# Tiles 4 to 15 of x arrive transposed and are normalized with broadcast mean and scale tiles (gated linear-attention block, one core)

## The chip, the core and the metric

The kernel runs on one core of a Trainium2 chip. Its engines are PE (TensorE, matmuls and transposes), DVE (VectorE), ACT (ScalarE), POOL (GpSimd) and SP (SyncE, which here issues DMAs). Each engine works through its own queue in order; they meet through semaphores. The metric is device time in microseconds (us) of one execution. A profile is one execution recorded by the hardware profiler; its clock starts at the span's start.

## The reference

Input x is 2048 rows of 576 features, float32. Cut to what matters:

```python
xn = (x - mean(x)) / sqrt(var(x) + 1e-5)          # per row
q, k, v = split(xn @ wqkv)                        # 32 heads of 18
pq, pk = phi(q), phi(k)                           # phi(t) = (t+1 if t > 0 else exp(t)) + 1e-6
kv, z = pk^T v, sum(pk)                           # per head, over all rows
s = ((pq @ kv) / (pq . z + 1e-6)) @ wo
g = silu((gelu(xn @ w_gate) * (xn @ w_up)) @ w_down)
out = x + s * g
```

## The kernel before

The 2048 rows are 16 tiles of 128 tokens, four to a block, four blocks (tb 0 to 3) in two halves s = 0 and 1. Matmuls contract over features, so the normalized x is needed with features on the partitions. The 576 features are two halves of 288, and a half is three groups of 128 columns: two whole ones, and one of 32 that the host repeats four times (`xe`). A float32 operand is kept as two float32r words, a high one (an ACT copy) and the rest (a DVE subtraction), in the tiles `xo`; the plain float32 values lie in `xf`, because sums of blocks are formed from them later.

The stages, in order of time: the tile loop over x (K and V by `x_mm` and `kv_tile`, tiles 0 to 7), the Q products of blocks 0 and 1 (`q_store`), tiles 8 to 15, Q of blocks 2 and 3 (`q_hold`), the attention output (`s_mm`), the gate and up matrices (a seven-product block scheme, `matrix`), and the down projection (`down_all`) with the gating of the output in its last passes. The order of every engine's queue is the order in which the program is written (`pin`).

What happens to tile n of x, by the names that the profile shows:

- `load_x` (L153) brings a pair of tiles from `xe`, tokens on partitions, 768 columns each, into slot b14 or b15. From tile 4 on it waits until the slot's last pair is read.
- `spread` (L162) takes mean and variance on DVE (`bn_stats`, `bn_aggr`), with Ln and Exp on ACT; `scales` (L177) refines the scale on DVE.
- `center` (L192) subtracts and scales the tile in place, one DVE instruction over 128x768.
- `turn` (L198) makes six PE transposes of 128x128 into two PSUM banks, `xt`.
- `place` (L207) makes the operand's high words from the banks on ACT, and the rests on DVE.
- `save` (L224) copies the same banks to `xf` on ACT.

In `kv_tile(t)` (L433) the PE order is `x_mm(t, 0)`, `turn(t + 1)`, `x_mm(t, 1)`, `x_mm(t, 2)`, `kv_mm(t - 1)`; then comes `x_mm(t + 1, 0)`, the first to read the new operand. Each `x_mm` is 14 matmuls, 7 for each half of the features. Of the 7, the first four read the high words and the fifth and sixth the rests. On DVE the order is `k_post(t, 0)` (e_k and pk, 128x416), `place`'s subtractions, `k_post(t, 1)`, and then the mean, scale and centering of a later tile.

The passage from tile 7 to tile 8 I call the turnover. Eight `q_store` and one shorter one follow each other there, each with two ACT instructions and one DVE instruction (`phi`, written e_q and ph in the profile), and between them the list `behind` (L1347) puts the statistics of tiles 8 to 11, the preparation of tile 8, and `form` (L1344) of the block sums T1, T3 and T2. One `form` is a 128x1536 ACT copy, a DVE subtraction of 128x1024 and one of 32x512 (written xo_T), and a DMA of 1280 KB to DRAM (kept_T). All three use slot b12, so a `form` starts when the DMA of the one before has been read out. T1 to T4 replace the tiles of `xf` in place, and tile 8's new `xf` tiles take the slots of T1 and T3.

At the start 34 transposes of the identity (`idle`, L1230) run on PE while the first tile is loaded and normalized. At the end (`down_all`, L1197 to L1219) the last pass runs tile by tile (j = 0 to 3), and `close_last` (L1134) adds the PSUM bank to the accumulator (DVE), applies Silu (ACT), multiplies, adds x (DVE), and stores. For j = 3 it does all this in two halves of 144 columns.

Of the kernel before, what the change touches and what calls it, by code (L numbers as in the profile page):

```python
# [8 lines left out]
F32 = mybir.dt.float32  # L9
# [7 lines left out]
P = 128  # L17
# [70 lines left out]


@with_exitstack  # L90
def block_kernel(ctx, tc, x, xe, wq_d, wkv_d, wo, wgu_d, wd_d, out):
    nc = tc.nc
    sb = ctx.enter_context(tc.tile_pool(name="sb", bufs=1))

# [3 lines left out]
    def bank(name):  # L98
        return ps.tile([P, 512], F32, tag="one", bufs=6, name=name)
# [4 lines left out]
    def big(i, shape, dt, name):  # L104
        return sb.tile(shape, dt, tag=f"b{i}", bufs=1, name=name)
# [15 lines left out]
    def act(*args, **kw):  # L121
        pin(nc.scalar.activation(*args, **kw))  # L122

    def vec(op, *args, **kw):
        pin(getattr(nc.vector, op)(*args, **kw))  # L125
# [7 lines left out]
    def dma(out, in_, eng=None):  # L133
        tc.keep_in_program_order((eng or nc.sync).dma_start(out=out, in_=in_))
# [18 lines left out]
    def load_x(n, k):  # L153

        if n % 2 == 0:
            xstat[n // 2] = big(14 + n // 2 % 2, [P, 2, 2, 3 * P], F32, f"x_{n}")
        dma(
            out=xstat[n // 2][:, n % 2 : n % 2 + k],
            in_=xe[n * P : (n + k) * P].rearrange("(t p) j d -> p t j d", p=P),
        )  # L160

    def spread(n0, n):  # L162

        bn = sb.tile([P, TT, 12], F32, tag="bn", bufs=2, name=f"bn_{n0}")
        mv = sb.tile([P, 2 * TT, 2], F32, tag="mv", bufs=4, name=f"mv_{n0}")
        for t in range(n):
            xs = xstat[(n0 + t) // 2][:, (n0 + t) % 2]
            for j in range(2):
                vec("bn_stats", out=bn[:, t, 6 * j : 6 * j + 6], in_=xs[:, j, 0:HALF])
            vec("bn_aggr", out=mv[:, t, :], in_=bn[:, t, :])  # L170
        st = sb.tile([P, 6, TT], F32, tag="st", bufs=4, name=f"st_{n0}")
        act(st[:, 0, 0:n], mv[:, 0:n, 1], AF.Ln, bias=eps_t)
        act(st[:, 2, 0:n], st[:, 0, 0:n], AF.Exp, scale=-0.5)
        vec("tensor_scalar", st[:, 1, 0:n], mv[:, 0:n, 1], LN_EPS, None, op0=ALU.add)
        mom[n0] = n, mv, st

    def scales(n0):  # L177

        n, mv, st = mom.pop(n0)
        v, r, c = (st[:, i, 0:n] for i in range(1, 4))  # L180
        if n == 1:
            vec("tensor_scalar", c, r, r, -0.5, op0=ALU.mult, op1=ALU.mult)
            vec("tensor_scalar", c, c, v, 1.5, op0=ALU.mult, op1=ALU.add)
            vec("tensor_scalar", c, c, r, None, op0=ALU.mult)
        else:
            vec("scalar_tensor_tensor", c, r, -0.5, r, op0=ALU.mult, op1=ALU.mult)
            vec("tensor_mul", c, c, v)
            vec("scalar_tensor_tensor", c, c, 1.5, r, op0=ALU.add, op1=ALU.mult)
        for t in range(n):
            scale_of[n0 + t] = mv[:, t, 0:1], c[:, t : t + 1]  # L190

    def center(n):  # L192

        xs = xstat[n // 2][:, n % 2]
        m, r = scale_of.pop(n)
        vec("tensor_scalar", xs, xs, m, r, op0=ALU.subtract, op1=ALU.mult)

    def turn(n, new=bank):  # L198

        xs = xstat[n // 2][:, n % 2]  # L200
        tiles = [new(f"xt_{n}_{j}") for j in range(2)]
        xts[n] = [t[:, 0 : 3 * P].rearrange("p (k t) -> p k t", k=3) for t in tiles]
        for j in range(2):
            for k in range(3):
                pin(nc.tensor.transpose(xts[n][j][:, k, :], xs[:, j, k * P : (k + 1) * P], ident))  # L205

    def place(n, js=(0, 1), words=(0, 1)):  # L207

        tb, t = divmod(n, TT)
        s, b = divmod(tb, 2)  # L210
        c = slice(t * P, (t + 1) * P)
        for j in js:
            nm = BS[b][j]
            if nm not in xo[s]:
                xo[s][nm] = big(2 * b + j, [P, 5, TBN], F32R, f"xo_{s}_{nm}")
            o, v = xo[s][nm], xts[n][j]
            if 0 in words:
                act(o[:, 0:3, c], v, AF.Copy)
            if 1 in words:
                vec("tensor_sub", o[:, 3:5, c], v[:, 0:2, :], o[:, 0:2, c].bitcast(F32))  # L220
                r = slice(KR, 2 * KR)
                vec("tensor_sub", o[r, 2, c], v[r, 2, :], o[r, 2, c].bitcast(F32))

    def save(n, js=(0, 1), last=True):  # L224

        tb, t = divmod(n, TT)
        s, b = divmod(tb, 2)
        for j in js:
            nm = BS[b][j]
            if t == 0:  # L230
                at_ = XM[s][nm]
                xf[s][nm] = (mid if at_ < 3 else big)(at_, [P, 3, TBN], F32, f"xf_{s}_{nm}")
            act(xf[s][nm][:, :, t * P : (t + 1) * P], xts[n][j], AF.Copy)
        if last:
            xts.pop(n)
# [841 lines left out]
    def acc_of(o):  # L1077
        i, j = ACCS[o]
        if i not in acc_t:
            acc_t[i] = big(i, [P, 2, TT, HALF], F32, f"acc_{i}")  # L1080
        return acc_t[i][:, j]
# [49 lines left out]
        vec("tensor_add", t[:, 0], t[:, 0], t[:, 1])  # L1131
        stores.append(lambda: dma(out=out[rows(j), cols], in_=t[:, 0]))

    def close_last(o, j, p, parts):  # L1134

        _, cols, rows = places(o)
        w = HALF // parts
        y, t, b = acc_of(o)[:, j], sxs[o][j], banks[p % 2][j]
        d = dict(PROD[p][3])[o]
        cs = [slice(i * w, (i + 1) * w) for i in range(parts)]  # L1140
        for c in cs:
            vec("tensor_add" if d > 0 else "tensor_sub", y[:, c], y[:, c], b[:, c])
            act(y[:, c], y[:, c], AF.Silu, scale=float(SIGN[o]))

        def rest():
            for c in cs:
                z = t[:, 0, c]
                vec("tensor_mul", z, y[:, c], z)
                vec("tensor_add", z, z, t[:, 1, c])
                dma(  # L1150
                    out=out[rows(j), cols.start + c.start : cols.start + c.stop], in_=z
                )

        return [rest]

# [17 lines left out]
    def down_all():  # L1173
        late = []
        last = NP - 1
        for u in range(NP * NU):
            p, k = divmod(u, NU)
            n = KT * p + 2 * k
            for at in sorted(events):
                if at <= H_END + n // 2:  # L1180
                    run_events(at)
            if p in LOADS and k < 3:
                load_reg(*LOADS[p], k)
            if k == 0:
                for o, e in ENDS.items():
                    if e == p:
                        load_sx(o)
            if k < 2:
                change(p + 1, k)
                if p in SHARED:  # L1190
                    make_words(p + 1, k)
            elif k < 4:
                make_words(p + 1, k - 2)
                if p + 1 in SHARED and p:
                    make_words(p + 2, k - 2)
            cut(u + 2)
            if p == last and k == 2:  # L1197
                break
            for kt in range(*UNITS[k]):
                down_mm(p, kt, range(TT))  # L1200
            load_unit(p + 1, k)
            run(stores)
            if k == 1 and p:
                read(p - 1)
                late += [
                    lambda o=o, j=j: close(o, j) for o, e in ENDS.items() if e == p - 1
                    for j in range(TT)
                ]
            else:
                run(late, 2)  # L1210
        run(late)
        run(stores)
        o = next(o for o, e in ENDS.items() if e == last)
        for j in range(TT):
            for kt in range(UNITS[2][0], KT):
                down_mm(last, kt, (j,))
            late += close_last(o, j, last, 2 if j == TT - 1 else 1)
            run(late, len(late) - 1)
        run(late)  # L1219

# [6 lines left out]
        ins=[], outs=[], act_func_set_id=LN_EXP,  # L1227
    )))
    first = [own_bank(f"idle_{i}") for i in range(2)]
    for i in range(34):  # L1230
        pin(nc.tensor.transpose(first[i % 2][:, 0:P], ident, ident))  # L1231
    load_x(0, 1)
    load_kv(0, 0)
# [110 lines left out]
    def form(nm):  # L1344
        keep(0, nm, build(0, nm, 12))

    behind = {  # L1347
        (0, 0): [lambda: kv_mm(N0 - 1), lambda: spread(N0, 2), lambda: difference(0, 3)],
        (0, 1): [lambda: scales(N0), lambda: center(N0), lambda: q_store(1, 4)],
        (0, 2): [lambda: form("T1")],  # L1350
        (0, 3): [lambda: turn(N0), lambda: place(N0)],
        (1, 0): [lambda: form("T3"), lambda: save(N0)],
        (1, 1): [lambda: center(N0 + 1), lambda: spread(N0 + 2, 2), lambda: scales(N0 + 2)],
        (1, 2): [lambda: form("T2")],
    }
    for tb in range(2):
# [140 lines left out]
```

## Time and profile before

| quantity | value |
|---|---|
| time, median of 3 runs | 1473.43 us (1472.06 to 1473.94) |
| time of the profiled execution | 1472.68 us |
| span of the profiled execution | 1470.9 us |
| PE busy | 1461.8 us |
| DVE busy | 1138.0 us |
| ACT busy | 572.0 us |
| POOL busy | 579.1 us |
| granted PE clock, share of full speed | 0.999 |

The execution's time is 1.8 us longer than its span, which runs from the first to the last recorded work. Busy times overlap, so they don't add up to the span. In a timeline row the first number is the start, the second how long the row lasted (several instructions of one kind are merged, with their count at the end, and may overlap), and the brackets tell the idle time before it and what ended it. In the chain of waits, each row is the work that the next row waited for.

### The profile page before, as it was taken

To read this page: it belongs to the slowest core of one execution; us is meant where nothing else is said; L and a number is where in the kernel's file an instruction comes from. 1 tells how busy PE (TensorE), PEld (TensorE's weight loads), DVE (VectorE), ACT (ScalarE), POOL (GpSimd) and SP (SyncE) were. 2 spreads that over 40 slices of the span, in tenths; PEclk is the share of its full clock that TensorE was granted. 3 is DMA by queue.
4 is the path that set the end of the run, shared out by engine and by line. 5 is a ranking of instruction groups with operands and counts; after the bars stand their busy time and mean duration, and the time that the engine had idled before them with its cause. 6 is when DMAs were issued, how large, how long until landed. Compare 5 with 4: busy or idle time off the path is not lost.

```text
span 1470.9 us, 21966 instructions
## 1 busy us (share of the span) xinstructions
PE 1461.8 (99%) x8184; PEld 1303.9 (89%) x8184; DVE 1138.0 (77%) x1581; ACT 572.0 (39%) x936; POOL 579.1 (39%) x513
## 2 busy tenths in 40 slices
PE   9999999999999999999999999999999999999998
PEld 8989989988888888888888888888889999999998
DVE  7566477466878788877778888778788978989888
ACT  5445355433222332223223223322335556455444
POOL 3332340125655667655674755757632000000000
PEclk9999999999999999999999999999999999999999
DMA  4435004442242323334153242423379888767886
GB/s 175 157 135 204 5 2 180 147 189 86 93 144 97 125 87 116 128 115 136 51 172 100 94 136 73 157 87 101 128 271 345 270 258 253 244 190 233 278 287 216
DMA packets 116148, 230.43 MB, mean 157 GB/s; under 512 B 10874, under 2 KB 44410, under 8 KB 113994
## 3 DMA queue, kind: packets, MB, share of 16 engines
q1 hardware_dynamic: 113386, 216.97, 44.0%
q0 software_dynamic: 2656, 12.06, 2.2%
q8 instruction: 65, 1.06, 0.3%
q14 instruction: 41, 0.34, 0.1%
HBM read 146.37 MB, written 82.58 MB: 156 GB/s over the span
## 4 chain that ended last, share of the span: by engine, by line
PE 96%; DVE 2%; issue 1%; DMA 0%; ACT 0%; POOL 0%; ACTq 0%; DVEq 0%; POOLq 0%
PE bd L128 23%; PE ga L769 16%; PE al L769 16%; PE de L769 16%; PE kv L128 8%; PE be L769 8%; PE s L128 4%; PE q L128 3%; PE kv_a L128 1%; PE xt L205 1%; DMA raw_h<-hs 0%; PE idle L1231 0%; PE d L128 0%; PE kw L128 0%; DVE acc L125 0%
## 5 line engine op out<-in xcount | busy, mean ns | idle before, releaser
L131 POOL TENSOR_TENSOR sm<-raw 128x384 f32<-128x384 f32 x72 | 75.2, 1044 | 152.0 <-DMA raw<-in_wgu_dram 107.4
L128 PE MATMUL kv<-wkv,xo_B 128*128 128x388 f32 (+2 forms) x658 | 127.9, 349 | 0.5 <-DVE xo_B L125 0.4
L128 PEld LDWEIGHTS kv<-wkv,xo_B 128*128 128x128 f32 x658 | 118.8, 188 | 2.4 <-DVE xo_B L125 0.7
L125 DVE TENSOR_TENSOR wa<-sm,wa 128x768 fp32r<-128x768 f32 x72 | 92.5, 1285 | 36.1 <-ACT wa L122 35.2
L128 PE MATMUL bd<-w_head,hi 128*128 128x288 f32 x516 | 118.0, 294 | 0.0
L125 DVE TENSOR_TENSOR wb<-raw,wb 128x256 fp32r<-128x256 f32 (+1 forms) x108 | 107.0, 991 | 7.3 <-ACT wb L122 5.8
L125 DVE TENSOR_TENSOR wa<-raw,wa 128x256 fp32r<-128x256 f32 x72 | 68.2, 947 | 50.7 <-ACT wa L122 49.6
L122 ACT ACTIVATE hi<-raw_h 128x1024 fp32r<-128x1024 f32 x59 | 62.4, 1059 | 90.0 <-PE bd L128 60.9
L128 PE MATMUL bd<-w_end,hi 128*128 128x288 f32 x448 | 89.8, 294 | 0.0
L122 ACT ACTIVATE spot_h<-spot_h 128x512 f32<-128x512 f32 x49 | 30.8, 633 | 151.4 <-DVE spot_h L125 151.4
L128 PEld LDWEIGHTS bd<-w_head,hi 128*128 128x128 f32 x516 | 87.0, 188 | 0.1
L125 DVE TENSOR_TENSOR raw_h<-raw_h,hi 128x1024 fp32r<-128x1024 f32 x59 | 71.9, 1223 | 16.7 <-ACT hi L122 16.7
L128 PE MATMUL bd<-w_end,raw_h 128*128 128x288 f32 x264 | 77.9, 295 | 0.0
L122 ACT ACTIVATE u<-al 128x512 f32<-128x512 f32 x72 | 41.0, 592 | 90.0 <-PE al L769 60.9
L122 ACT ACTIVATE wa<-sm 128x1152 fp32r<-128x1152 f32 x36 | 41.8, 1161 | 84.8 <-PE de L769 84.8
L128 PEld LDWEIGHTS bd<-w_end,hi 128*128 128x128 f32 x448 | 71.9, 188 | 0.0
L128 PE MATMUL bd<-beside,raw_h 128*128 128x288 f32 x240 | 70.9, 295 | 0.0
L131 POOL TENSOR_TENSOR spot_h<-spot_h,spot_h 128x512 f32<-128x512 f32 x45 | 62.3, 1390 | 2.9 <-DVE spot_h L125 2.4
L769 PE MATMUL ga<-xo_B,wb 128*128 128x512 f32 x252 | 63.0, 389 | 0.0
L769 PE MATMUL al<-xo_B,wa 128*128 128x512 f32 x252 | 63.0, 389 | 0.0
L769 PE MATMUL al<-xr_B,wb 128*128 128x512 f32 x252 | 63.0, 389 | 0.0
L769 PE MATMUL al<-xr_B,wa 128*128 128x512 f32 x252 | 63.0, 389 | 0.0
(261 smaller groups left out, 4066.5 us busy)
## 6 DMA issues: line engine op xcount, KB each, us to landing
raw_h<-hs SPq DMA_DIRECT2D x176, 256.0 KB
raw<-in_wgu_dram SPq DMA_DIRECT2D x36, 768.0 KB
hs<-spot_h SPq DMA_DIRECT2D x90, 256.0 KB
hs<-spot_g SPq DMA_DIRECT2D x80, 256.0 KB
b<-in_wd_dram SPq DMA_DIRECT2D x42, 432.0 KB
hs<-spot_m SPq DMA_DIRECT2D x38, 256.0 KB
raw_g<-hs SPq DMA_DIRECT2D x22, 256.0 KB
kept_T<-xo_T SPq DMA_DIRECT2D x4, 1280.0 KB
```

The costliest lines, as they stand in the source:

```text
L122: pin(nc.scalar.activation(*args, **kw))
L125: pin(getattr(nc.vector, op)(*args, **kw))
L128: pin(nc.tensor.matmul(*args, **kw))
L131: pin(getattr(nc.gpsimd, op)(*args, **kw))
L205: pin(nc.tensor.transpose(xts[n][j][:, k, :], xs[:, j, k * P : (k + 1) * P], ident))
L769: nc.tensor.matmul(o, w[0:rows, wi, :], xop[0:rows, xi, :], start=(start and n == 0), stop=(n == len(PASSES) - 1), skip_group_check=True,)
```

## The change

For tiles 4 to 15 the host passes a second copy of x, `xt`, in which each tile stands with features on the partitions. `load_x` now loads both forms, 576 columns of the plain rows (for the statistics) and 768 columns of `xt`, in two DMAs. `center`, `save` and the six transposes fall away for these tiles. `turn` transposes two columns instead, the mean and the scale of the tile's tokens, each broadcast to 128x128, so that one PSUM bank `ms` holds both with tokens along the free axis. `normalize` subtracts the mean tile in place (128x768), multiplies by the scale tile into `xf` (twice 128x384), and makes the words from `xf` (`to_operand`, two ACT copies and four DVE subtractions). Tiles 0 to 3 stay as they were.

In the turnover, `form("T1")` moves from behind `q_store(0, 2)` to behind `q_store(0, 1)`, ahead of the shorter `q_store(1, 4)`, and tile 8 is prepared behind `form("T3")` instead of ahead of `q_store(1, 0)`.

The identity transposes at the start become 28. For j = 3 of the last pass, the accumulator is added to the PSUM bank ahead of the remaining matmuls of the pass, which then accumulate on top of it. Silu reads the bank, and the rest is done in one piece of 288 columns.

```diff
     def load_x(n, k):
         if n % 2 == 0:
-            xstat[n // 2] = big(14 + n // 2 % 2, [P, 2, 2, 3 * P], F32, f"x_{n}")
-        dma(
-            out=xstat[n // 2][:, n % 2 : n % 2 + k],
-            in_=xe[n * P : (n + k) * P].rearrange("(t p) j d -> p t j d", p=P),
-        )
+            shape = [P, 2, 2, 3 * P] if n < TT else [P, 2, D + 6 * P]
+            xstat[n // 2] = big(14 + n // 2 % 2, shape, F32, f"x_{n}")
+        t = xstat[n // 2][:, n % 2 : n % 2 + k]
+        if n < TT:
+            dma(out=t, in_=xe[n * P : (n + k) * P].rearrange("(t p) j d -> p t j d", p=P))
+        else:
+            dma(out=t[:, :, 0:D], in_=x[n * P : (n + k) * P].rearrange("(t p) d -> p t d", p=P))
+            dma(out=t[:, :, D:], in_=xt[n : n + k].rearrange("t p m -> p t m"))
...
     def turn(n, new=bank):
         xs = xstat[n // 2][:, n % 2]
+        if n >= TT:
+            xts[n] = t = bank(f"ms_{n}")
+            for i, v in enumerate(scale_of.pop(n)):
+                pin(nc.tensor.transpose(
+                    t[:, i * P : (i + 1) * P], v.to_broadcast([P, P]), ident
+                ))
+            return
...
+    def normalize(n, s, b, c):
+        ms = xts.pop(n)
+        xs = xstat[n // 2][:, n % 2, D:].rearrange("p (k t) -> p k t", k=6)
+        m, r = (ms[:, None, i * P : (i + 1) * P] for i in range(2))
+        vec("tensor_sub", xs, xs, m.to_broadcast([P, 6, P]))
+        for j, nm in enumerate(BS[b]):
+            if nm not in xo[s]:
+                xo[s][nm] = big(2 * b + j, [P, 5, TBN], F32R, f"xo_{s}_{nm}")
+                new_plain(s, nm)
+            vec(
+                "tensor_mul", xf[s][nm][:, :, c], xs[:, 3 * j : 3 * j + 3],
+                r.to_broadcast([P, 3, P]),
+            )
+        for nm in BS[b]:
+            to_operand(xo[s][nm], xf[s][nm], c)
...
+    def add_in(o, j, p):
+        b = banks[p % 2][j][:, 0:HALF]
+        vec("tensor_add" if dict(PROD[p][3])[o] > 0 else "tensor_sub", b, b, acc_of(o)[:, j])
...
+        if added:
+            act(y, b, AF.Silu, scale=float(SIGN[o] * d))
+        else:
+            vec("tensor_add" if d > 0 else "tensor_sub", y, y, b)
+            act(y, y, AF.Silu, scale=float(SIGN[o]))
...
         o = next(o for o, e in ENDS.items() if e == last)
+        add_in(o, TT - 1, last)
         for j in range(TT):
             for kt in range(UNITS[2][0], KT):
                 down_mm(last, kt, (j,))
-            late += close_last(o, j, last, 2 if j == TT - 1 else 1)
+            late += close_last(o, j, last, j == TT - 1)
...
-    for i in range(34):
+    for i in range(28):
...
     behind = {
         (0, 0): [lambda: kv_mm(N0 - 1), lambda: spread(N0, 2), lambda: difference(0, 3)],
-        (0, 1): [lambda: scales(N0), lambda: center(N0), lambda: q_store(1, 4)],
-        (0, 2): [lambda: form("T1")],
-        (0, 3): [lambda: turn(N0), lambda: place(N0)],
-        (1, 0): [lambda: form("T3"), lambda: save(N0)],
-        (1, 1): [lambda: center(N0 + 1), lambda: spread(N0 + 2, 2), lambda: scales(N0 + 2)],
+        (0, 1): [
+            lambda: scales(N0), lambda: form("T1"), lambda: q_store(1, 4),
+        ],
+        (0, 3): [lambda: turn(N0)],
+        (1, 0): [lambda: form("T3"), lambda: place(N0)],
+        (1, 1): [lambda: spread(N0 + 2, 2), lambda: scales(N0 + 2)],
         (1, 2): [lambda: form("T2")],
     }
```

More of the change, by code (lines that the diff above doesn't have):

```diff
@@ L90, in block_kernel @@
 @with_exitstack
-def block_kernel(ctx, tc, x, xe, wq_d, wkv_d, wo, wgu_d, wd_d, out):
+def block_kernel(ctx, tc, x, xe, xt, wq_d, wkv_d, wo, wgu_d, wd_d, out):
     nc = tc.nc
@@ L168, in spread @@
             for j in range(2):
-                vec("bn_stats", out=bn[:, t, 6 * j : 6 * j + 6], in_=xs[:, j, 0:HALF])
+                src = xs[:, j, 0:HALF] if n0 < TT else xs[:, j * HALF : (j + 1) * HALF]
+                vec("bn_stats", out=bn[:, t, 6 * j : 6 * j + 6], in_=src)
             vec("bn_aggr", out=mv[:, t, :], in_=bn[:, t, :])
@@ L200, in turn @@
         xs = xstat[n // 2][:, n % 2]
+        if n >= TT:
+            xts[n] = t = bank(f"ms_{n}")
[3 more added lines that the diff above has]
+                ))
+            return
         tiles = [new(f"xt_{n}_{j}") for j in range(2)]
@@ L205, in turn, with new_plain @@
                 pin(nc.tensor.transpose(xts[n][j][:, k, :], xs[:, j, k * P : (k + 1) * P], ident))
+    def new_plain(s, nm):
+        at_ = XM[s][nm]
+        xf[s][nm] = (mid if at_ < 3 else big)(at_, [P, 3, TBN], F32, f"xf_{s}_{nm}")
+    def normalize(n, s, b, c):
[13 more added lines that the diff above has]
+            to_operand(xo[s][nm], xf[s][nm], c)
     def place(n, js=(0, 1), words=(0, 1)):
@@ L211, in place @@
         c = slice(t * P, (t + 1) * P)
+        if n >= TT:
+            normalize(n, s, b, c)
+            return
         for j in js:
@@ L227, in save @@
         s, b = divmod(tb, 2)
+        if n >= TT:
+            return
         for j in js:
@@ L230, in save @@
             if t == 0:
-                at_ = XM[s][nm]
-                xf[s][nm] = (mid if at_ < 3 else big)(at_, [P, 3, TBN], F32, f"xf_{s}_{nm}")
+                new_plain(s, nm)
             act(xf[s][nm][:, :, t * P : (t + 1) * P], xts[n][j], AF.Copy)
@@ L1132, in close, with close_last @@
         stores.append(lambda: dma(out=out[rows(j), cols], in_=t[:, 0]))
-    def close_last(o, j, p, parts):
+    def add_in(o, j, p):
+        b = banks[p % 2][j][:, 0:HALF]
+        vec("tensor_add" if dict(PROD[p][3])[o] > 0 else "tensor_sub", b, b, acc_of(o)[:, j])
+    def close_last(o, j, p, added):
         _, cols, rows = places(o)
-        w = HALF // parts
-        y, t, b = acc_of(o)[:, j], sxs[o][j], banks[p % 2][j]
+        y, t, b = acc_of(o)[:, j], sxs[o][j], banks[p % 2][j][:, 0:HALF]
         d = dict(PROD[p][3])[o]
[L1140 to L1143, printed above, removed]
-        def rest():
[L1146 to L1152, printed above, removed]
+        if added:
[3 more added lines that the diff above has]
+            act(y, y, AF.Silu, scale=float(SIGN[o]))
+        def rest():
+            z = t[:, 0]
+            vec("tensor_mul", z, y, z)
+            vec("tensor_add", z, z, t[:, 1])
+            dma(out=out[rows(j), cols], in_=z)
         return [rest]
@@ L1482 @@
     for name, a in (
-        ("x", xs), ("xe", xe), ("wq", wq), ("wkv", wkv), ("wo", A_wo), ("wgu", wgu), ("wd", wd)
+        ("x", xs), ("xe", xe[0 : 4 * P]), ("xt", xt), ("wq", wq), ("wkv", wkv), ("wo", A_wo), ("wgu", wgu), ("wd", wd)
     ):
```

1 line of the change is left out of this document (added).

## The prediction

> **What bounds the kernel now.** I read the page's busy times and its chain first, then PE's own waits, then the groups of instructions by shape, and last the timeline of the places that the change touches.
>
> ```profile
> span 1470.9 us, 21966 instructions
> ...
> PE 1461.8 (99%) x8184; PEld 1303.9 (89%) x8184; DVE 1138.0 (77%) x1581; ACT 572.0 (39%) x936; POOL 579.1 (39%) x513
> ...
> PE 96%; DVE 2%; issue 1%; DMA 0%; ACT 0%; POOL 0%; ACTq 0%; DVEq 0%; POOLq 0%
> ```
>
> PE is busy for 1461.8 of 1470.9 us, and 96% of the chain that ended last is PE. It is idle for 9.1 us: some 5.3 follow its last matmul (the tail's rows below), and of the rest these are the waits that bear on the change:
>
> ```profile
> PE idle L1231 <- POOL ident masks.py:199: 1.8, 1, 1.8
> ...
> PE kv L128 <- DVE xo_B L125: 0.4, 1, 0.4
> ...
> PE xt L205 <- DVE x L125: 0.2, 1, 0.2
> ```
>
> The first is the start, before the first instruction. So an instruction taken out of PE's queue shortens the program by its pace, as long as no other engine then comes too late. That is the question for each part.
>
> **Transposes.** Their group among PE's instructions by shape:
>
> ```profile
> L205 PE MATMUL xt<-ident,x 128*128 128x128 f32 x96 | 13.2, 274 | 0.8 <-issue 0.5 <-DVE x L125 0.2
> ```
>
> 96 transposes (16 tiles of six) keep PE busy for 13.2 us, 0.1375 us each at their pace; the 274 ns of one overlaps its neighbours. Twelve tiles lose four each: 48 x 0.1375 = **6.6 us**. The two that stay in a tile read a broadcast column, which no row shows. Bounds: no dearer, or paced by the 188 ns of the slowest common weight load:
>
> ```profile
> L128 PEld LDWEIGHTS kv<-wkv,xo_B 128*128 128x128 f32 x658 | 118.8, 188 | 2.4 <-DVE xo_B L125 0.7
> ```
>
> That would be 24 x 0.05 = 1.2 us dearer. I take 0, since their shape and type are those of the transposes.
>
> **DVE in an ordinary tile.** The group rows for the instruction that goes (the centering, L125's TENSOR_SCALAR on x) and for subtractions of two tensors:
>
> ```profile
> L125 DVE TENSOR_TENSOR xo_B<-xt,xo_B 128x256 fp32r<-128x256 f32 x32 | 13.5, 422 | 3.0 <-ACT xo_B L122 2.3
> ...
> L125 DVE TENSOR_TENSOR xf_B<-xf_B,xf_B 128x1536 f32<-128x1536 f32 x6 | 12.6, 2098 | 0.3
> L125 DVE TENSOR_SCALAR x<-x,mv,st 128x768 f32<-128x768 f32 x16 | 10.9, 680 | 0.6
> ```
> ```profile
> L125 DVE TENSOR_TENSOR raw_h<-raw_h,hi 128x1024 fp32r<-128x1024 f32 x59 | 71.9, 1223 | 16.7 <-ACT hi L122 16.7
> ```
>
> From 422 ns at 256 elements to 1223 at 1024 is 1.04 ns an element, so 128x768 comes to 0.96 us and 128x384 to 0.56. In a tile DVE gains 0.96 + 2 x 0.56 = 2.08 us and loses the 0.68 of the centering; ACT loses the two copies of `save`. Whether PE then waits, the rows of tile 4 show: its turn, the end of `k_post` ahead of it on DVE, and the first matmuls that read it.
>
> ```profile
> 42.75 0.82 PE L205 MATMUL xt<-ident,x 128*128 128x128 f32 x6
> ```
> ```profile
> 43.46 0.58 DVE L125 TENSOR_SCALAR pk<-kv 128x416 f32<-128x416 f32 x1
> ```
> ```profile
> 49.49 2.88 PE L128 MATMUL kv<-wkv,xo_B 128*128 128x416 f32 x14
> ```
>
> DVE is free at 44.04. The subtraction lasts to 45.0, the first multiplication to 45.6, its ACT copy (0.49, as 128x384 takes in the turnover's rows) to 46.1. The first matmul would start at 49.49 - 0.55 (four transposes fewer) = 48.94. So 2.8 us of other matmuls cover the new work and I cost it at nothing; each microsecond beyond that cover would cost 11, once for every tile but 8.
>
> The Trainium skill (VectorE: DVE Perf Modes, section Why PSUM operands drop a tier) says that an operand in PSUM holds a float32 instruction at one element a cycle. That speaks against this change, for the centering it removes does 768 elements in 0.68 us, less than the 0.96 interpolated. At the centering's pace a multiplication would cost some 0.42 instead of 0.56, the chain of the turnover below would be about 1.0 us shorter, and the sum better by as much. By the rule, the rows of two tensors are the ones to go by, and the sum stays as it is.
>
> **Loads.** A pair now moves 576 KB more and takes one more SP issue. In the late tiles SP waits in `load_x` for DVE's multiplications instead of the transposes, some 3 us longer; queued behind it are stores of ph and kept_T, which nobody reads soon. For tiles 12 and 13, the issue and the first reader:
>
> ```profile
> 124.79 0.86 SPq L134 DMA_DIRECT2D x<-in_xe_dram  x1
> ```
> ```profile
> 140.38 0.82 DVE L125 BATCH_NORM_STATS2 bn<-x 128x6 f32<-128x288 f32 x2
> ```
>
> 15.6 us lie between: no cost. Were they used up, tile 12 would be late by the excess.
>
> **The turnover.** Here other work already ends last. The chain of waits before:
>
> ```profile
> 118.18 2.61 PE kv L128 x14
> ...
> 121.52 0.68 DVE xo_T L125
> ...
> 122.23 0.69 DVE ph L125
> 122.93 0.50 DVE e_k L125
> 123.42 0.50 DVE pk L125
> ```
>
> It leaves PE for DVE: T2's subtraction, ph, `k_post`, and then tile 9's words. That is PE's 0.4 + 0.2 = 0.6 us of waiting in the second fence. What holds T2 back stands further up, in ACT's queue, DVE's, and SP's:
>
> ```profile
> 95.32 0.64 ACT L122 ACTIVATE e_q<-e_q 128x512 f32<-128x512 f32 x1
> ...
> 106.10 0.63 ACT L122 ACTIVATE e_q<-e_q 128x512 f32<-128x512 f32 x1
> 109.30 1.49 ACT L122 ACTIVATE xo_T<-xf_B 128x1536 fp32r<-128x1536 f32 x1 [2.57 <-DMA kept_T<-xo_T]
> ...
> 112.84 0.49 ACT L122 ACTIVATE xf_B<-xt 128x384 f32<-128x384 f32 x1 [1.68 <-DVE xo_T L125]
> ```
> ```profile
> 110.82 1.92 DVE L125 TENSOR_TENSOR xo_T<-xf_B,xo_T 128x1024 fp32r<-128x1024 f32 x2 [4.03 <-ACT xo_T L122]
> ...
> 115.17 0.81 DVE L125 BATCH_NORM_STATS2 bn<-x 128x6 f32<-128x288 f32 x2
> ...
> 117.19 0.17 DVE L125 TENSOR_SCALAR st<-mv 128x2 f32<-128x2 f32 x1
> ```
> ```profile
> 103.41 0.32 SPq L134 DMA_DIRECT2D kept_T<-xo_T  x1
> ```
>
> T3's copy at 109.30 had waited 2.57 us for T1's DMA, issued at 103.41: a trip of 5.9. In the changed kernel T1 starts behind the e_q that ends at 95.96: copy 1.49, DVE 1.92 and a bit, issue near 99.6, read out by 105.5. So the trip no longer holds T3; ACT's queue does, until e_q of `q_store(1, 0)` ends at 106.73 - 0.55 (tile 8's shorter turn) = 106.2. T3 comes 3.1 us earlier. But tile 8's normalization now stands behind it, in front of everything else. In before's clock: T3's copy to 107.7, DVE to 109.6; subtraction and two multiplications to 111.6; the second ACT copy 0.49 and its words 0.75 (two of the four subtractions) to 112.9; ph 0.69 to 113.6; statistics of tiles 10 and 11, 2.02 (from 115.17 to 117.19), to 115.6; then on ACT the Ln and Exp 0.5, two e_q of 0.6, T2's copy 1.49, to 118.8; DVE 1.92 to 120.7; ph to 121.4; `k_post` 1.0 to 122.4; tile 9's subtraction and multiplication 1.52 to 123.9; ACT 0.49 to **124.4**. PE without waits: tile 9's first matmul stood at 118.18 + 2.61 + 2.61 x 388/412 (the last product's narrower columns) = 123.2; two shorter turns make it **122.1**. PE waits 2.3 us where it waited 0.6: a loss of **1.7 us**. From tile 10 on the ordinary cover holds again. Bounds: no wait at all (0.6 better than before), or a wait of 3.6 (3.0 worse than before), with DVE's pieces slowed as the 128x1536 rows are, 2.10 on average against 1.75 in the one below:
>
> ```profile
> 93.75 1.75 DVE L125 TENSOR_TENSOR xf_B<-xf_B,xf_B 128x1536 f32<-128x1536 f32 x1
> ```
>
> **Start.** The last idle transposes, then DVE's rows: the centering of tile 0, tile 1's weights and words; then PE ahead of tile 2's turn.
>
> ```profile
> 7.23 0.82 PE L1231 MATMUL idle<-ident 128*128 128x128 f32 x6
> ```
> ```profile
> 6.41 0.68 DVE L125 TENSOR_SCALAR x<-x,mv,st 128x768 f32<-128x768 f32 x1
> ...
> 11.18 1.61 DVE L125 TENSOR_TENSOR wkv<-rw,wkv 128x832 fp32r<-128x832 f32 x2
> ...
> 13.46 1.51 DVE L125 TENSOR_TENSOR xo_B<-xt,xo_B 128x256 fp32r<-128x256 f32 x4 [0.67 <-ACT xo_B L122]
> ```
> ```profile
> 25.68 0.54 issue
> ```
>
> The last six idle transposes take 0.82 us and tile 0 is ready at 7.09, before 7.23, so its turn comes 0.82 earlier. At 25.68 PE waits for tile 2, at the end of a nearly full DVE queue. That queue moves as far as tile 1's words do, and they can't start before DVE is free at 12.79, 0.67 before 13.46. I take **0.65**; bounds 0 and 0.82.
>
> **Tail.** DVE's adds, and PE's first matmul for j = 3:
>
> ```profile
> 1462.29 0.81 DVE L125 TENSOR_TENSOR acc<-acc,bd 128x288 f32<-128x288 f32 x2
> ...
> 1465.60 0.52 DVE L125 TENSOR_TENSOR acc<-acc,bd 128x144 f32<-128x144 f32 x2 [0.17 <-PE bd L128]
> ...
> 1467.80 0.31 DVE L125 TENSOR_TENSOR sx<-sx 128x144 f32<-128x144 f32 x1
> ```
> ```profile
> 1463.42 0.29 PE L128 MATMUL bd<-beside,hi 128*128 128x288 f32 x1
> ```
>
> DVE is nearly full from 1462.3 on and ends at 1468.1; the last store ends the span. The early add goes ahead of j = 0's, from 1462.3 to 1462.7, and delays the adds behind it by 0.4. PE reaches j = 3 at 1463.42, so 0.7 us cover it; without them PE would wait for it. Out go the two late adds (0.52), their wait (0.17), and, with one piece for two, some 0.3. Net **0.6**; bounds 0 (the last store is larger) and 0.9.
>
> **The sum.** 6.6 + 0.65 + 0.6 - 1.7 = 6.15 us. The profiled execution's own time is 1472.68, the span and 1.8 around it, so 1466.5. It lies 0.75 below the median of the runs, 1473.43; the forecast for a median is **1467.3**.
>
> **Rivals.**
> - *The turnover is cured.* T3's 3.1 us suffice and PE doesn't wait: 1467.3 - 2.3 = 1465.0. For it: the wait that held T3 goes. Against: what is put behind T3 is all in DVE's one queue.
> - *The turnover is worse and the transposes dearer*, both upper bounds: 1467.3 + 1.3 + 1.2 = 1469.8. For it: T1's trip has only 0.7 us of reserve, and POOL adds ph beside DVE there. Against: one of the two bounds has no row of its own.
> - *Every tile waits*, the slower side. If DVE took far longer over a broadcast PSUM operand, the first operand of each tile, priced at 1.52 us, would outlast its cover. That begins at 2.8 times my price; at 3.6 times the delay is 3.95, 1.15 over the cover, and costs 11 x 1.15 = 12.7: 1480.0. Against: no row of two tensors is that slow.
> - *The change doesn't do what it says*: PE's transposes hide a wait that comes to light when they go, and the time stays at 1473.4. Against: 0.6 us of waiting is all that PE shows at these tiles.
>
> **Chances.** The forecast 0.50, cured 0.20, worse 0.14, every tile waits 0.09, nothing gained 0.07. About 0.2% (2.9 us) is what a measurement can tell from no change. Faster takes in the first two and nearly all of the third, 0.80; same 0.11; slower 0.09. The range, 1464.5 to 1470.6, holds the first three cases with the bounds of their costs.
>
> **What would show it.** Right: PE's idle rows shorter by six, 24 transposes of ms at the pace of xt, a wait of 2 to 3 us on xo_B once near 122 and none at other tiles, DVE's last row ending some 0.6 sooner behind PE's last matmul. Wrong: waits on xo_B at many tiles, a wait on x's loads, or transposes of ms that are slower than those of xt.

## The result, and the profile after

| quantity | before | after |
|---|---|---|
| time, median of 13 runs each | 1472.30 us (1471.28 to 1473.94) | 1469.94 us (1467.89 to 1471.75) |
| ratio, 95% interval | | 0.998 (0.9972 to 0.9987) |
| profiled execution: time, span | 1472.68, 1470.9 us | 1467.89, 1466.2 us |
| PE busy, DVE busy in it | 1461.8, 1138.0 us | 1454.2, 1152.6 us |

The change makes the kernel faster by 2.4 us of the medians, 0.16%: the forecast direction, within the range, but 2.6 us above the forecast time and not beyond the 0.2% that was set as the bound for calling it faster. Of the rivals, the one nearest to it is the worse turnover with dearer transposes, 1469.8. The profiled execution gained twice as much, 4.8 us; it is one of the two fastest of the 13, and why that matters comes out below. Three lines of the page, in the form that was shown of before:

```profile
span 1466.2 us, 21844 instructions
...
PE 1454.2 (99%) x8130; PEld 1296.8 (88%) x8130; DVE 1152.6 (79%) x1602; ACT 561.1 (38%) x911; POOL 578.2 (39%) x513
...
PE 95%; DVE 3%; ACT 1%; issue 1%; POOL 0%; ACTq 0%; DVEq 0%; POOLq 0%
```

PE lost 7.6 us of busy time, the span only 4.7: PE's idle time rose from 9.1 to 12.0 us. Its waits (engine, tile and line, what released it; us in all, count, longest) say where:

```profile
PE kv L128 <- ACT xo_B L122: 2.6, 1, 2.6
...
PE xt L218 <- PE idle L1272: 0.8, 1, 0.8
```

One wait of 2.6 us stands at tile 9's first product, and no other tile waits for its operand. The second row is the start, where tile 0's turn now waits for the centering instead of standing in the queue.

**The transposes.** PE's instructions on the two broadcast columns, and DVE's of the normalization (each row: x count, busy us, mean ns, idle before):

```profile
L210 PE MATMUL ms<-ident,mv 128*128 128x128 f32 x12 | 3.3, 272 | 0.0
L210 PE MATMUL ms<-ident,st 128*128 128x128 f32 x12 | 3.3, 276 | 0.1
```
```profile
L125 DVE TENSOR_TENSOR xf_B<-x,ms 128x384 f32<-128x384 f32 x24 | 12.2, 550 | 0.4
L125 DVE TENSOR_TENSOR x<-x,ms 128x768 f32<-128x768 f32 x12 | 11.4, 951 | 0.3
```

A broadcast column costs what a plain transpose did (274 ns). The two DVE instructions were priced at 0.96 and 0.56 us and took 0.951 and 0.550. What a tile of x saves is best read in the chain of waits, where each row is the time that the work held the path. Before, then after, from one `turn` to the next:

```profile
42.91 0.66 PE xt L205 x6
43.57 5.10 PE kv L128 x28
48.67 0.88 PE kv_a L128 x8
...
52.37 0.66 PE xt L205 x6
```
```profile
42.11 0.22 PE ms L210 x2
42.33 5.11 PE kv L128 x28
47.44 0.88 PE kv_a L128 x8
...
51.13 0.22 PE ms L210 x2
```

The period falls from 9.46 to 9.02 us. All of it is in the transposes, 0.66 us for six and 0.22 for two, so 0.11 us each, and the matmuls between have the same times. Twelve tiles make 12 x 0.44 = 5.3 us.

**The turnover.** The rows of PE, ACT and DVE around tile 9's first product (in brackets the idle time before and what ended it):

```profile
122.47 2.90 PE L128 MATMUL kv<-wkv,xo_B 128*128 128x416 f32 x14 [2.63 <-ACT xo_B L122]
```
```profile
103.66 1.48 ACT L122 ACTIVATE xo_T<-xf_B 128x1536 fp32r<-128x1536 f32 x1
...
121.89 0.99 ACT L122 ACTIVATE xo_B<-xf_B 128x384 fp32r<-128x384 f32 x2 [4.13 <-DVE xf_B L125]
```
```profile
116.65 1.92 DVE L125 TENSOR_TENSOR xo_T<-xf_B,xo_T 128x1024 fp32r<-128x1024 f32 x2 [1.35 <-ACT xo_T L122]
118.60 0.69 DVE L125 TENSOR_SCALAR ph<-q 128x512 f32<-128x512 f32 x1
...
120.31 0.95 DVE L125 TENSOR_TENSOR x<-x,ms 128x768 f32<-128x768 f32 x1
121.30 1.02 DVE L125 TENSOR_TENSOR xf_B<-x,ms 128x384 f32<-128x384 f32 x2
```

The order is the one that was forecast: T2's subtraction, ph, `k_post`, tile 9's subtraction and multiplications, its copy, PE. T3's copy no longer waits for a DMA. By then this kernel is 2.5 us ahead of before's clock (the first e_q stands at 87.92 against 90.42), so T3 started at 106.16 on that clock, and 106.2 was forecast.

**The end and the middle.** PE's last matmul and DVE's last instruction:

```profile
1460.65 0.29 PE L128 MATMUL bd<-w_end,raw_g 128*128 128x288 f32 x1
```
```profile
1462.21 0.46 DVE L125 TENSOR_TENSOR sx<-sx 128x288 f32<-128x288 f32 x1
```

DVE ends 1.73 us behind PE's last matmul, 0.8 sooner than before (2.55), but the store that ends the span takes 3.5 us from there where the smaller one took 2.8. So the tail went from 5.34 to 5.26 us in this pair. The start of the down projection moved more than the end did, as the chain shows:

```profile
1092.62 138.23 PE bd L128 x1044
...
1230.87 6.83 DMA raw_h<-hs
```
```profile
1088.77 203.25 PE bd L128 x1535
```

At its start the kernel is 3.85 us ahead (1092.62 - 1088.77). Another 0.7 come up inside the down projection, 372.2 us against 372.9 to PE's last matmul, where before's chain left PE for a DMA at 1230.87 and after's runs on. The one edit in that stretch, the early add at its end, is not the cause: e3 and e8 below have the old end and take 372.2 too, while e4, the kernel before with another start, takes 372.9. In before and e4 PE waits there once for the words of raw_h, 0.2 us, and the weight loads wait 0.8 to 1.0 us for them; what makes them late was not tried. So of the profiled 4.8 us, about 4 belong to the edits: 0.77 at the start (the products behind tile 3's turn begin at 33.34 against 34.11), 5.3 from transposes, 2.0 lost to the wait (2.63 instead of 0.6), 0.1 at the tail: 4.2. The medians show 2.4. The question for the experiments was where the rest goes.

### The profile page after: what moved, and what is told of

Read it like the earlier page. It is cut to its first block, busy times and chain, and to the rows that moved or that the text cites. A ratio compares the mean times of both kernels' runs of the same rounds, so it can differ in the third digit from the quotient of the medians.

```text
span 1466.2 us, 21844 instructions
## 1 busy us (share of the span) xinstructions
PE 1454.2 (99%) x8130; PEld 1296.8 (88%) x8130; DVE 1152.6 (79%) x1602; ACT 561.1 (38%) x911; POOL 578.2 (39%) x513
## 4 chain that ended last, share of the span: by engine, by line
PE 95%; DVE 3%; ACT 1%; issue 1%; POOL 0%; ACTq 0%; DVEq 0%; POOLq 0%
PE bd L128 24%; PE al L807 16%; PE ga L807 16%; PE de L807 16%; PE be L807 8%; PE kv L128 7%; PE s L128 4%; PE q L128 3%; PE kv_a L128 1%; DVE sx L125 1%; PE d L128 0%; PE kw L128 0%; PE idle L1272 0%; PE b L128 0%; ACT xo_T L122 0%
## 5 line engine op out<-in xcount | busy, mean ns | idle before, releaser
L125 DVE TENSOR_TENSOR wb<-raw,wb 128x256 fp32r<-128x256 f32 (+1 forms) x108 | 101.0, 935 | 7.4 <-ACT wb L122 5.8
L807 PE MATMUL de<-xo_T,wa 128*128 128x512 f32 x252 | 63.0, 389 | 0.0
L807 PE MATMUL de<-xo_T,wb 128*128 128x512 f32 x252 | 63.0, 389 | 0.0
```

What stands on the lines that cost most here:

```text
L807: nc.tensor.matmul(o, w[0:rows, wi, :], xop[0:rows, xi, :], start=(start and n == 0), stop=(n == len(PASSES) - 1), skip_group_check=True,)
```

## The experiments

Each was timed beside runs of the kernel before on the same chip, whose medians in three batches were 1472.22, 1472.53 and 1472.70 us. The edits are made to the changed kernel unless said otherwise.

**e1: the turnover mended.** T2 is formed a tile later, behind tile 9's words, and T4 moves with it.

```diff
         (1, 1): [lambda: spread(N0 + 2, 2), lambda: scales(N0 + 2)],
-        (1, 2): [lambda: form("T2")],
     }
...
+        if n == N0:
+            ends.append(lambda: form("T2"))
-        if n == N0 + 1:
+        if n == N0 + 2:
             ends.append(lambda: form("T4"))
```

> The changed kernel with the forms of T2 and T4 one step later: T2 behind tile 8's products instead of ahead of the last q_store, T4 behind tile 10's instead of tile 9's, so that 3.4 us of ACT and DVE work no longer stand ahead of tile 9's words. Theory A (the wait of 2.63 us in the profile costs what it lasts and nothing else): the wait is gone, PE's row of it shows less than 0.5, and the median falls by 2 to 2.7 us below the changed kernel's 1469.9, to 1467.2 to 1467.9. Rival C (PE's wait also lets the granted clock fall in most executions, which the one profiled did not show): the median falls by 3.5 us or more, to 1466.4 or less, and the runs lie closer together. Rival D (the same work only makes a later tile wait): a wait on xo_B at tile 10 or 11 of 1 us or more, median within 1 us of 1469.9.

Measured: 1465.72 us (1465.05 to 1466.35), ratio 0.9955 (0.9943 to 0.9968). PE's waits:

```profile
PE xt L218 <- issue: 0.5, 1, 0.5
...
PE kv L128 <- ACT xo_B L122: 0.2, 1, 0.2
```

The wait shrank by 2.4 us, the median by 4.2. The wait seems to cost more than its own length. The two profiled executions, in which PE's granted clock is 1.00 in all tiles, lie 2.4 us apart (1465.52 against 1467.89), which is the wait and no more.

**e2: 34 idle transposes.** The start as it was before.

```diff
-    for i in range(28):
+    for i in range(34):
```

> The changed kernel with 34 identity transposes at the start as before, nothing else. Theory A (start worth what the profile shows, 0.77 us): the first matmul of the first tile comes 0.6 to 0.9 us later and the median is 0.5 to 1.0 us above the changed kernel's 1469.9. Rival B (with 28, PE is granted its full clock later in most executions, which costs more than the start gains): the median is 1 us or more below 1469.9.

Measured: 1471.04 us (1467.99 to 1471.78), ratio 0.9985 (0.9976 to 0.9994). That is 1.1 us above the changed kernel, within both kernels' spread, so it doesn't price the start. What the run showed lies elsewhere. Its 11 times fall into two groups, five from 1467.99 to 1468.72 us and six from 1471.04 to 1471.78. Its profile has the same wait as the changed kernel and another length of the product behind it:

```profile
123.34 4.25 PE L128 MATMUL kv<-wkv,xo_B 128*128 128x416 f32 x14 [2.62 <-ACT xo_B L122]
```

These 14 matmuls took 2.90 us above. PE by stretches of 2 us (window, length, PE busy and count, PE's granted clock, share and rate of the DMAs), here and then in the changed kernel:

```profile
120.00:122.00 2.00, 0.71 (x5) 1.00 0.97 410
122.00:124.00 2.00, 0.66 (x2) 0.72 0.90 366
124.00:126.00 2.00, 2.00 (x8) 0.50 0.74 169
126.00:128.00 2.00, 2.00 (x12) 0.93 1.04 397
```
```profile
120.00:122.00 2.00, 0.00 (x0) 1.00 0.98 410
122.00:124.00 2.00, 1.53 (x8) 1.00 0.85 240
124.00:126.00 2.00, 2.00 (x14) 1.00 0.87 220
```

While PE still waited, the granted clock began to fall, to 0.50 here; it stayed at 1.00 in the one profile of the changed kernel. PE's busy time times the share of the clock that was missing gives 0.66 x 0.28 + 2 x 0.50 + 2 x 0.07 = 1.3 us lost.

**e3: the old tail.** `close_last` and the last pass as before: no early add, j = 3 in two halves.

```diff
-        add_in(o, TT - 1, last)
...
-            late += close_last(o, j, last, j == TT - 1)
+            late += close_last(o, j, last, 2 if j == TT - 1 else 1)
```

> The changed kernel with the end as before: no early add into the bank, j = 3 closed in two halves. Theory A (the tail gained DVE time and gave it back in the larger last store, 5.26 us from PE's last matmul to the span's end against 5.34): median within 0.3 us of the changed kernel's 1469.9, span's end 5.2 to 5.5 us behind PE's last matmul. Rival (my forecast's 0.6 us for the tail): median 0.5 to 0.9 us above.

Measured: 1470.71 us (1468.56 to 1472.60), ratio 0.9989 (0.9980 to 0.9997). From PE's last matmul to the span's end there are 5.78 us against 5.26, more than was expected of a tail that gives its gain back. The median, 0.8 us higher, can't be put down to the tail alone, since most of these executions have a lower mean clock (0.997 or 0.998). In the profile, the fall of the clock began within the wait of 2.63 us and lasted longer than in e2:

```profile
120.00:122.00 2.00, 0.00 (x0) 0.96 0.98 410
122.00:124.00 2.00, 1.53 (x4) 0.50 0.75 235
124.00:126.00 2.00, 2.00 (x7) 0.50 0.93 258
126.00:128.00 2.00, 2.00 (x8) 0.50 0.97 389
128.00:130.00 2.00, 2.00 (x11) 0.83 0.05 18
```

By the same sum that is 3.1 us (the first row holds no matmul), more than the wait itself.

**e4: 28 idle transposes in the kernel before.** Its one edit is `range(34)` to `range(28)`.

> The kernel before with 28 identity transposes instead of 34, nothing else. Theory A: 0.6 to 0.9 us faster than before (median near 1471.6), with the transposes of tile 0 starting near 7.2 us. Rival B (clock granted later): no faster than before, or slower, with a pace of the first matmuls above that of before.

Measured: 1471.51 us (1470.72 to 1472.41), ratio 0.9995 (0.9986 to 1.0004): 0.7 us by the medians, and an interval that takes in no change.

**e5: the wait filled.** 22 idle transposes of the identity go between the two products, where PE waits. The wait for tile 9 itself is left as it is.

```diff
+    def fill():
+        t = bank("fill")
+        for i in range(22):
+            pin(nc.tensor.transpose(t[:, i % 2 * P : (i % 2 + 1) * P], ident, ident))
...
+        if n == N0:
+            ends.append(fill)
```

> The changed kernel, its turnover as it is, with 22 identity transposes put on PE where it waits for tile 9 (22 x 0.11 = 2.4 us of the 2.63), so that PE is idle for only some 0.2 us there while tile 9 comes no sooner. Theory C (the idle time lets the granted clock fall to half for 1 to 6 us in most executions): the clock stays at 1.0 from 120 to 130, the first product of tile 9 takes 2.9 us and not 4.3 to 5.2, and the median falls by 1 to 2 us below the changed kernel's 1469.9, its runs within 2 us of each other. Rival (the clock falls there for another reason, such as the DMA traffic at that time): windows at 0.5 stay and the median is within 0.5 us of 1469.9.

Measured: 1468.97 us (1467.95 to 1469.67), ratio 0.9975 (0.9965 to 0.9985). Timeline and stretches:

```profile
119.86 2.56 PE L1405 MATMUL fill<-ident 128*128 128x128 f32 x22
122.66 2.91 PE L128 MATMUL kv<-wkv,xo_B 128*128 128x416 f32 x14 [0.23 <-ACT xo_B L122]
```
```profile
120.00:122.00 2.00, 2.00 (x21) 1.00 1.06 445
122.00:124.00 2.00, 1.77 (x11) 1.00 0.86 278
```

The product starts as late as it did (122.66 against 122.47) and PE does nothing useful meanwhile, yet the time doesn't rise; the median falls by 1.0 us. The mean granted clock is 0.999 or more in all eight executions, where 6 of the changed kernel's 13 have 0.998. The intervals of e5 and of the changed kernel overlap, so the gain in the median isn't shown by this pair alone; that the clock stays up is.

**e6: six broadcast transposes a tile, in e1.** Each of the two columns is turned three times. The four additional results are not read.

```diff
-            for i, v in enumerate(scale_of.pop(n)):
+            for i, v in enumerate(3 * scale_of.pop(n)):
+                i = i if i < 4 else i - 2
```

> The kernel with the mended turnover (median 1465.7) and again six transposes a tile for tiles 4 to 15: the two of ms are made three times, the copies going to unused columns of the bank. So 48 more transposes, nothing else. Theory A (a transpose costs PE 0.108 us at its pace, as tile periods of 9.45 and 9.02 us say): 5.0 to 5.4 us slower, near 1470.9. Rival (my forecast's 0.1375): 6.4 to 6.8 us slower, near 1472.3.

Measured: 1470.48 us (1469.63 to 1471.01), ratio 0.9984 (0.9975 to 0.9993), 4.8 us above e1 for 48 transposes, or 4.4 when each is set against its own batch's before: 0.09 to 0.10 us each. The chain agrees with before's, 0.66 us for the six:

```profile
42.17 0.66 PE ms L211 x6
42.83 5.06 PE kv L128 x28
```

This gives the transposes their price in the time of the kernel, without the turnover's wait: 4.4 to 4.8 us by the medians, 5.3 by the chain, not 6.6.

**e7: 34 idle transposes, in e1.** The edit of e2.

> The kernel with the mended turnover (median 1465.7) and 34 identity transposes instead of 28. Theory A: 0.6 to 0.9 us slower. Rival B (28 delay the clock): no slower, or faster.

Measured: 1466.21 us (1465.59 to 1466.80), ratio 0.9955 (0.9943 to 0.9968). Six idle transposes fewer are worth 0.5 us by the medians, and the ratio is e1's: small, of the forecast sign, and not told apart from nothing.

**e8: the old tail, in e1.** The edit of e3.

> The kernel with the mended turnover (median 1465.7) and the end as before: no early add into the bank, j = 3 in two halves. If the tail's gain is given back in the last store: within 0.3 us. If the forecast's 0.6 is right: 0.4 to 0.8 us slower, and the span's end 5.7 us or more behind PE's last matmul, as in the changed kernel with the old tail (5.8), instead of 5.3.

Measured: 1466.17 us (1465.89 to 1466.41), ratio 0.9955 (0.9943 to 0.9968): 0.45 us above e1 by the medians, or 0.1 when each is set against its own batch's before. From PE's last matmul to the span's end it has 5.76 us, 0.5 more than e1's 5.29, as was expected if the forecast's 0.6 is right. But the kernel before takes only 5.34, and e4 5.37. Over all profiles the old tail takes 5.34 to 5.78 (before, e3, e4, e8; mean 5.56) and the new one 5.22 to 5.52 (after, e1, e2, e5, e6, e7, e9, e10; mean 5.30). So the edit gives 0.1 to 0.5 us, some 0.25 by these means.

**e9: T1 formed where it was.** Behind `q_store(0, 2)` again, with the rest of the changed kernel.

```diff
-            lambda: scales(N0), lambda: form("T1"), lambda: q_store(1, 4),
+            lambda: scales(N0), lambda: q_store(1, 4),
         ],
+        (0, 2): [lambda: form("T1")],
```

> The changed kernel with T1's form back in its old place, behind q_store(0, 2), so that T1's DMA trip of 5.9 us again ends after ACT is ready for T3. If the forecast's step on T1 is right (its early start lets T3 come some 3 us sooner): T3's copy starts 2.5 to 3.5 us later than in the changed kernel (103.66 there) behind a DMA wait, PE's wait for tile 9 grows from 2.6 to 5 to 6 us, and with an idle time that long the granted clock is at half behind it in the profile; median 1472.5 to 1475. Rival (DVE's queue alone sets the wait, T1's place is indifferent): wait 2.5 to 3 us and median within 1 us of 1469.9.

Measured: 1471.93 us (1470.77 to 1473.49), ratio 0.9994 (0.9985 to 1.0003). ACT's row of T3, and PE's of tile 9:

```profile
105.46 1.49 ACT L122 ACTIVATE xo_T<-xf_B 128x1536 fp32r<-128x1536 f32 x1 [1.37 <-DMA kept_T<-xo_T]
```
```profile
124.27 5.22 PE L128 MATMUL kv<-wkv,xo_B 128*128 128x416 f32 x14 [4.11 <-ACT xo_B L122]
```

The DMA of T1 holds T3 back again, by 1.8 us (105.46 against 103.66), and PE waits 1.5 us longer, less than was expected of it. The clock fell again while PE waited:

```profile
122.00:124.00 2.00, 0.00 (x0) 0.76 1.07 451
```

The median is 2.0 us above the changed kernel's. That T1's earlier start frees T3 is right, and it is worth 1.5 us of waiting.

**e10: 22 idle transposes, in e1.** Once more `range(28)`, now to `range(22)`.

> The kernel with the mended turnover (median 1465.7 on one chip, 6.5 below before) with 22 identity transposes. If the start is bound by DVE's centering from 28 down (at full clock 28 end at 6.5, at half clock at 7.6, centering at 7.1): 0 to 0.4 us faster. Rival B in a stronger form (too few transposes leave the clock at half in the first products): the first product of tile 0 and those after it show windows at half speed pace, and the median is 0.5 us or more slower.

Measured: 1465.22 us (1464.88 to 1465.66), ratio 0.9949 (0.9936 to 0.9961), the fastest of all kernels here, 7.5 us below before. Its start:

```profile
1.76 4.64 PE L1272 MATMUL idle<-ident 128*128 128x128 f32 x22 [1.76 <-POOL ident masks.py:199]
7.25 0.84 PE L218 MATMUL xt<-ident,x 128*128 128x128 f32 x6 [0.86 <-PE idle L1272]
```

PE waits 0.86 us for tile 0's centering, so fewer idle transposes can bring no more. The spreads of e10 and e1 overlap, so the 0.5 us between their medians is not told from nothing.

**e11: the last store in halves, in e1.** Only the multiplication, the addition of x and the store of j = 3 are done in two pieces of 144 columns.

```diff
-            z = t[:, 0]
-            vec("tensor_mul", z, y, z)
-            vec("tensor_add", z, z, t[:, 1])
-            dma(out=out[rows(j), cols], in_=z)
+            n = 2 if added else 1
+            for i in range(n):
+                c = slice(i * HALF // n, (i + 1) * HALF // n)
...
```

> The kernel with the mended turnover, the early add and one Silu for j = 3, but its multiplication, addition and store in two halves of 144 columns. If the store of 288 columns (3.5 us from DVE's last row to the span's end) against 144 (2.8) is what took the tail's gain: span's end 4.8 to 5.1 us behind PE's last matmul instead of 5.3, median 0.2 to 0.5 us lower, 6.7 to 7.0 below before. If the store's time doesn't go by its size: 5.5 to 5.7, median 0.2 to 0.4 higher.

Measured: 1466.63 us (1465.00 to 1466.74), ratio 0.9956 (0.9942 to 0.9969), and 5.34 us from PE's last matmul to the span's end, between what the two readings expected. It decides nothing; a gain there is not seen. From DVE's last row to the span's end it has 3.3 us with the store of 144 columns, so that the size alone sets this time is not shown.

## Why the prediction was partly right

**What bounds the kernel: right.** PE stays busy for 99% of the span, and each transpose added or removed showed at its pace (e6).

**Transposes: 6.6 forecast, 5.3 in the chain, 4.4 to 4.8 in e6's medians.** The step that failed is "96 transposes keep PE busy for 13.2 us, 0.1375 us each at their pace". Busy time of a group runs to the end of its last matmul, and the next group's first matmul starts before that. Before's own timeline has the row behind the one that was quoted at 42.75:

```profile
43.33 5.35 PE L128 MATMUL kv<-wkv,xo_B 128*128 128x412 f32 x28
```

The next product starts 0.58 us behind the six, not 0.82, which is 0.097 each. The chain's 0.66 for six says the same, more simply. So 1.3 to 2.2 us of the shortfall are this term. That the broadcast column costs nothing more was right.

**DVE and ordinary tiles: right.** The interpolated prices hold within 10 ns, and no tile but 9 waits. The Trainium skill's statement that was weighed there (VectorE: DVE Perf Modes, section Why PSUM operands drop a tier), one element a cycle for an operand in PSUM, agrees: 951 ns for 768 elements, where the centering that went took 680. But the 1223 ns for 1024 elements of raw_h and hi, the row of two tensors that the forecast went by, have the same pace with no operand in PSUM, so these runs don't tell whether PSUM or the second tensor sets it.

**Loads: right.** No wait for x appears on PE.

**Turnover: the wait was right, its price was not.** 2.3 us was forecast, 2.63 came, T3 started at the forecast moment, and T1's new place does what it was said to do (e9). What failed is "a loss of 1.7 us": it takes the wait at its length. PE's clock can fall to half during it and stay there behind it. The numbers for that, over all executions: in the kernels without the long wait (before, e1, e4 to e8, e10, e11) the mean granted clock is 0.999 to 1.000 every time; in the four with it (after, e2, e3, e9) it is 0.997 or 0.998 in 28 of 45. A mean of 0.999 alone is no sign of such a fall, because the mean takes in the span's end, where the clock falls too once PE has nothing left (last section). The changed kernel's own 13 executions sort themselves by it: three at 1.000 took 1467.89, 1467.89 and 1468.62 us, the ten at 0.998 or 0.999 took 1469.21 to 1471.75. The middle of the first three and of the other ten lie 2.1 us apart, and 0.1 to 0.2% of 1454 us of busy PE is 1.5 to 2.9. e1, without the wait, gains 1.8 us beyond the wait's 2.4 in the medians and nothing beyond it in the two profiles at full clock, and e5, with the idle time filled, shows no fall of the clock. That the wait lets the clock fall is shown; that this makes up all of the 1.8 us in the medians is a sum that fits, not a separate measurement.

**Start: 0.65 forecast, 0.2 to 0.8 found.** The profiles of before and after give 0.77; e4 gives 0.7 by the medians, e7 0.5, or 0.2 when each is set against its own batch's before, and neither ratio tells it from nothing; e2's 1.1 mixes executions with and without a fall of the clock. The step assumed 0.1375 us for each of the last six, and their pace changes from execution to execution (below).

**Tail: 0.6 forecast, 0.1 to 0.5 found.** DVE did end 0.8 us sooner. What was named as a bound and left out of the sum, "the last store is larger", took the rest by the clock: from DVE's last row to the span's end 3.5 us passed instead of 2.8 to 3.2. Whether the store's size is the reason, e11 leaves open.

**The sum, again.** 4.4 to 5.3 for transposes, about 0.5 at the start, 0.1 to 0.5 at the tail, minus 2.0 for the wait make 3.0 to 4.3; about 1.5 to 2 for the clock leave 1.0 to 2.8, and 2.4 was measured. The forecast's base hid a part of the miss: the median of three runs that it started from, 1473.43, is 1.1 us above the median of 13, so that the gain was 3.8 us short of the 6.15 forecast, and the time only 2.6 us above. Among the rivals, "the turnover is cured" was priced at 1465.0; this kernel isn't it, but e1 is that case, at 1465.72. "The turnover is worse and the transposes dearer" was priced at 1469.8, next to the 1469.94 measured, but by terms that did not come true: a transpose of ms costs no more than one of xt, and the wait was 2.63 us, not 3.6. So the mechanism of the forecast held but for the clock, its terms were too good by 3 to 5 us together, and that the time still lies in the range, which reaches to 1470.6, is owed to the bounds of that rival and is partly luck.

## What to carry to other kernels

An instruction that leaves a full PE queue is worth about its spacing on the chain (0.11 us here, 0.09 to 0.10 by e6's medians), not its group's busy time divided by the count, which holds the overlap as well. A wait that is new on PE and lasts as long as the 2.6 us here should be priced at its length plus a stretch at half clock, and looked for in several executions, since one profile can miss it. Moving such a wait's cause by one tile (T2 here) was worth 4.2 us, more than the 2.4 of the change that brought it. Keeping PE at work through the wait kept the clock up, and brought about 1 us, not told from nothing.

## What the hardware did that was not expected

**PE's clock falls in a wait of 2.6 us, but not every time.** Of three profiles with a wait of 2.62 or 2.63 us, one kept the clock at 1.00. In the others it fell to 0.50, 2.2 us into the wait in e2 and 2.0 in e3, and in the wait of 4.11 us of e9 it fell 2.9 us in (read in windows of 0.2 us). From the missing shares in these rows (in e9 the three behind the one shown have 0.50, 0.50 and 0.53), the stretch at 0.50 lasted 3.4 us in e2 and 6.8 us in e3 and in e9, twice as long. The span's end shows the same in all 13 profiles: the clock falls to 0.50 at some time between 2.0 us (before) and 5.2 us (e10) after PE's last matmul. In the kernels whose waits in the tiles stayed at 0.6 us or less, no profile shows a fall before the end, and no execution a mean clock below 0.999. The Trainium skill (TensorE: Matmul & The Clock Gate, section What's actually happening) says that the clock is halved after an idle window of about 3.4 us and that this window runs freely. That it depends on the execution agrees with the second; that 2.0 to 2.2 us of idle PE were enough in e2 and e3 is less than the first names, and the measurement decides.

**Transposes alone keep the clock up.** In e5 PE did nothing but transposes for 2.56 us, and the clock stayed at 1.00; no execution's mean is below 0.999.

**The first transposes run at changing paces.** PE's idle transposes in the profiles of the changed kernel, of e1 and of e7:

```profile
1.75 4.74 PE L1272 MATMUL idle<-ident 128*128 128x128 f32 x28 [1.75 <-POOL ident masks.py:199]
```
```profile
1.75 5.87 PE L1272 MATMUL idle<-ident 128*128 128x128 f32 x28 [1.75 <-POOL ident masks.py:199]
```
```profile
1.75 5.57 PE L1272 MATMUL idle<-ident 128*128 128x128 f32 x34 [1.75 <-POOL ident masks.py:199]
```

The same 28 took 4.74 and 5.87 us, and 34 took 5.57. So a profile of one execution can't give the price of a few of them; by how much the first product moves depends on the start that it happened to get.
